# Block-causal attention with a rational feed-forward: q split compactly and placed by transfers, weights rebuilt as float32, four planner numbers

## The chip, the cores and the metric

The kernel runs on one core of a Trainium2 chip. The metric is the device time of one execution in microseconds; times of a version are given as the median of several runs. The engines are PE (TensorE, matmuls; PEld is its weight loading), DVE (VectorE), ACT (ScalarE), POOL (GpSimd) and SP (SyncE), which here only issues the transfers. Each engine works through its own queue of instructions in order.

## The reference, cut to what matters

Attention over 8 batches and 8 heads, 576 tokens, head size 64, with a mask by blocks of 64 tokens; its output, 4608 tokens by 512, goes through a feed-forward with a rational function between two matmuls. All results are float32, and the weights arrive as 64-bit floats.

```
scores = (q @ k.T) / 8, masked where block(i) < block(j)
attn = exp(scores - rowmax) / (rowsum + 1e-9)
x = (attn @ v), heads side by side          # 4608 x 512
h = x @ w_in                                # 4608 x 2048
g = (a0 + a1 h + a2 h^2 + a3 h^3) / (1 + |b0||h| + |b1|h^2 + 1e-6)
out = g @ w_out                             # 4608 x 512
```

## The kernel before

**Precision.** Every float32 operand of a matmul is held as two float32r tiles, a high part (a rounding copy on ACT) and a low part (the rest, by a subtraction on DVE or POOL). A product is three matmuls: high by high, high by low and low by high.

**Attention.** The 64 heads are worked in 32 pairs p. `load` (lines 326 to 341) brings a pair's q, k and v in; `prep` (359 to 385) transposes q and k on PE into a PSUM bank and splits them. For q the two heads go into a block-diagonal tile `qbd` (two of them, alternating), head 0 in partitions 0 to 63 and columns 0 to 63 of each block, head 1 in the other quarter, so that one matmul gives the scores of both heads; the zeros are written once, at lines 316. That takes, for each of q's two parts, an operation of 64 partitions by 512 for each head and a tail of 64 by 64 for each (L348 on ACT for high, L351 on DVE for low). A pair has ten score steps (d, j), ten steps k of a counter that runs through all pairs. At step k `scores` (410) makes the scores on PE and their negative maximum on DVE (L421). `expo` (426), emitted ALAG2 steps later, takes the exponential on ACT (L434), and scales the rows on POOL (L442, L447) after a reciprocal on DVE. `transp` (450), TLAG steps later, transposes the weights of attention on PE (L456) and splits them (L459, L460). `pv` (462), TLAG + 1 and + 2 steps behind a pair's last score step, multiplies with v (L487), rounds the result into the tile `xh` (ACT, L475 and L489) and the rest into `xl` (DVE), moves one half of `xh` across partitions by a transfer into `xt` (L491), adds it on POOL (L494) and stores the two parts to `xscr` in DRAM. For the next pair, OFFS gives the steps behind a pair's first score step at which `load` and the two calls of `prep` are emitted. PSUM has five banks for scores, transposes and results together.

**Weights.** 32 pieces of 128 by 512 are converted by `place` (109 to 140), 20 for the first part of the feed-forward (tiles stay in SBUF) and 12 for the second (high and low parts go to DRAM by L139 and L140 and come back at L583). A piece arrives as pairs of 32-bit words w0, w1. ACT takes the absolute value of w1 as a float (L120), POOL clamps it from below (L121), DVE shifts, masks and joins words in five operations (L123, L125, L128, L129, L130), ACT converts and copies, POOL multiplies.

**Feed-forward.** `Ffn` works 256 tokens at a time in its first part (`ph` 0, ten of the 16 blocks of w_in and w_out, five units a chunk) and 512 tokens in its second. A unit is 24 matmuls with w_in (L198), the rational function on ACT, POOL and DVE (L205 to L231), and 12 or 24 matmuls with w_out (L248). Its input comes back from `xscr` through SP (L181).

**What sets the order.** The program text is emitted step by step: at each attention step the weight pieces due by a table (lines 555, 562), then as many half units as a planner allows. A batch counts as ready `LAST = TLAG + 6` steps after its last step (line 557); the planner spreads the half units linearly up to U1, which is the ready work less HOLD (559, 569). A scheduler of the framework then sorts each engine's queue by its own estimate of times, so the queues do not follow the text exactly. After the last attention step the attention's buffers are freed, the second part's weights are loaded (L583), and the rest of the feed-forward runs alone.

## Time and profile before

| | |
|---|---|
| median of 3 runs | 1394.38 us (1388.48, 1394.38, 1395.79) |
| profiled execution | 1391.85 us, span in the profile 1390.1 us |
| mean granted PE clock | 0.948 |
| busy: PE, PEld | 1264.8 us (91%), 1113.6 us (80%) |
| busy: DVE, ACT, POOL | 1083.2 us (78%), 912.9 us (66%), 959.4 us (69%) |
| DMA | 153.52 MB, 199507 packets, 128480 of them under 512 bytes |

A row of the groups reads: line, engine, operation, output tile <- inputs, shape, count | busy us, mean ns of one | idle time of the engine just before, and what ended it. A row of the waits reads: who waited, for what: us in total, times, longest. Matmuls are pipelined and their ends are modelled, so a busy PE may still not be at its peak. The span falls into an opening without feed-forward, up to about 142 us, a middle in which attention and feed-forward are mixed, a short passage at 970 to 1005 us, and the rest of the feed-forward.

### The profile page before, as it was taken

What the parts mean: (1) busy time and instruction counts of PE and PEld (TensorE: products, weight loads), DVE (VectorE), ACT (ScalarE), POOL (GpSimd) and SP (SyncE); (2) the same over time, 40 slices, a digit from 0 to 9 for tenths busy, and PEclk for the clock granted to TensorE, in tenths of its full rate; (3) what the DMA queues carried; (4) which work ended last, traced back from release to release, by engine and by line L of the source; (5) the groups of instructions that cost most, each with busy time, mean ns of one, the idle gap of its engine ahead of it and who ended that gap; (6) DMA issues with size and microseconds to landing.
All of it is one profiled execution on the core that took longest, in us unless ns stands there. A gap on an engine that the chain in (4) does not pass through costs nothing.

```text
span 1390.1 us, 22425 instructions
## 1 busy us (share of the span) xinstructions
PE 1264.8 (91%) x7352; PEld 1113.6 (80%) x7352; DVE 1083.2 (78%) x2080; ACT 912.9 (66%) x2154; POOL 959.4 (69%) x1080
## 2 busy tenths in 40 slices
PE   6766799899989898999899999999799999999997
PEld 5656688788878787888888889898689888888885
DVE  8999878788777889778887888887287776666674
ACT  6676767676666767668687777776256655565553
POOL 5998867687666777677776777776376655656654
PEclk9776899999999999999999999999899999999998
DMA  5455333345243433334323324322712243333332
GB/s 144 137 148 167 101 100 105 97 115 159 73 121 82 120 105 99 107 88 137 104 77 102 87 67 122 92 80 68 287 31 81 75 134 121 121 122 121 121 113 84
DMA packets 199507, 153.52 MB, mean 110 GB/s; under 512 B 128480, under 2 KB 167392, under 8 KB 199392
## 3 DMA queue, kind: packets, MB, share of 16 engines
q1 hardware_dynamic: 199328, 152.09, 37.6%
q8 instruction: 59, 0.97, 0.3%
q14 instruction: 56, 0.46, 0.1%
q0 software_dynamic: 64, 0.00, 0.0%
HBM read 98.57 MB, written 44.04 MB: 103 GB/s over the span
## 4 chain that ended last, share of the span: by engine, by line
PE 55%; DVE 17%; POOL 10%; ACT 8%; DMA 5%; issue 4%; SPq 1%; POOLq 0%; DVEq 0%; ACTq 0%
PE h L198 21%; PE o L248 20%; PE o L487 5%; PE s L420 4%; PE t L456 2%; DVE ptrl L460 2%; DVE nm L421 2%; POOL p L447 2%; ACT p L434 2%; POOL u L208 2%; DMA xt<-xh 2%; DVE v L222 1%; DVE u L221 1%; DVE s L223 1%; POOL v L207 1%
## 5 line engine op out<-in xcount | busy, mean ns | idle before, releaser
L198 PE MATMUL h<-x,wih 128*128 128x256 f32 (+1 forms) x1872 | 422.6, 316 | 20.2 <-DMA x<-xscr 10.3
L198 PEld LDWEIGHTS h<-x,wih 128*128 128x128 f32 x1872 | 319.1, 196 | 45.1 <-DMA x<-xscr 11.7
L198 PE MATMUL h<-x,wil 128*128 128x256 f32 (+1 forms) x936 | 293.9, 314 | 0.0
L231 POOL TENSOR_TENSOR gl<-s,gh 128x512 fp32r<-128x512 f32 x144 | 189.8, 1319 | 89.4 <-ACT gh L230 88.9
L447 POOL TENSOR_SCALAR p<-p,rc 128x576 f32<-128x576 f32 (+8 forms) x288 | 199.2, 703 | 68.6 <-DVE rc L443 57.5
L248 PE MATMUL o<-woh,gl 128*128 128x512 f32 x576 | 234.0, 406 | 10.5 <-POOL gl L231 10.0
L248 PE MATMUL o<-woh,gh 128*128 128x512 f32 x576 | 229.2, 398 | 0.0
L248 PE MATMUL o<-wol,gh 128*128 128x512 f32 x576 | 228.4, 397 | 0.0
L434 ACT ACTIVATE p<-s,nm 128x288 f32<-128x288 f32 (+4 forms) x320 | 160.4, 505 | 70.3 <-DVE nm L421 42.3
L208 POOL TENSOR_TENSOR u<-v,u 128x512 f32<-128x512 f32 x144 | 191.4, 1329 | 9.5
L198 PEld LDWEIGHTS h<-x,wil 128*128 128x128 f32 x936 | 182.5, 195 | 8.6
L207 POOL TENSOR_SCALAR v<-u,bab 128x512 f32<-128x512 f32 x144 | 122.0, 847 | 94.2 <-ACT u L205 91.8
L421 DVE TENSOR_REDUCE nm<-s 128x1 f32<-128x288 f32 (+4 forms) x320 | 142.7, 450 | 41.8 <-PE s L420 39.6
L209 DVE TENSOR_TENSOR s<-s,h 128x512 f32<-128x512 f32 x144 | 98.3, 683 | 97.7 <-ACT s L206 96.5
L460 DVE TENSOR_TENSOR ptrl<-t,ptrh 128x384 fp32r<-128x384 f32 (+1 forms) x320 | 147.2, 481 | 18.1 <-ACT ptrh L459 16.8
L459 ACT CAST ptrh<-t 128x384 fp32r<-128x384 f32 (+1 forms) x320 | 126.3, 430 | 49.6 <-PE t L456 49.1
L456 PE MATMUL t<-ident,p 128*128 128x128 f32 x800 | 134.5, 291 | 25.0 <-DVE ptrl L460 13.8
L215 ACT ACTIVATE v<-u,qcb 128x512 f32<-128x512 f32 x144 | 104.6, 726 | 74.4 <-POOL u L208 73.7
L230 ACT CAST gh<-s 128x512 fp32r<-128x512 f32 x144 | 89.4, 624 | 87.3 <-DVE s L223 85.1
L205 ACT ACTIVATE u<-h 128x512 f32<-128x512 f32 x144 | 86.2, 599 | 89.7 <-PE h L198 82.7
L248 PEld LDWEIGHTS o<-woh,gl 128*128 128x128 f32 x576 | 110.5, 192 | 33.9 <-POOL gl L231 14.3
L456 PEld LDWEIGHTS t<-ident,p 128*128 128x128 f32 x800 | 100.8, 148 | 43.3 <-issue 7.2
(94 smaller groups left out, 2688.7 us busy)
## 6 DMA issues: line engine op xcount, KB each, us to landing
x<-xscr SPq DMA_DIRECT2D x56, 256.0 KB, 3.7
xt<-xh SPq DMA_DIRECT2D x64, 144.0 KB, 2.4
xscr<-xh SPq DMA_DIRECT2D x64, 144.0 KB, 2.4
xscr<-xl SPq DMA_DIRECT2D x32, 288.0 KB, 2.3
pscr<-os SPq DMA_DIRECT2D x18, 512.0 KB, 2.8
pt<-pscr SPq DMA_DIRECT2D x18, 512.0 KB, 4.2
out_dram<-os SPq DMA_DIRECT2D x18, 512.0 KB, 3.0
qr<-in_q_dram SPq DMA_DIRECT2D x64, 128.0 KB, 2.5
```

The costliest lines, as they stand in the source:

```text
L198: nc.tensor.matmul(h[:, j, :], lhsT=w[:, dc, fs], rhs=xs[dc][:, hl, :], start=(dc == 0 and i == 0), stop=(dc == 3 and i == 2))
L207: nc.gpsimd.tensor_scalar(out=vt, in0=ut, scalar1=b1, scalar2=b0, op0=ALU.mult, op1=ALU.add)
L208: nc.gpsimd.tensor_tensor(out=ut, in0=vt, in1=ut, op=ALU.mult)
L215: nc.scalar.activation(out=vt, in_=ut, func=AF.Ln, bias=qcb)
L231: nc.gpsimd.tensor_tensor(out=gl.rearrange("p j t -> p (j t)"), in0=st, in1=gh.rearrange("p j t -> p (j t)").bitcast(F32), op=ALU.subtract)
L248: nc.tensor.matmul(self.o[m], lhsT=g[:, j, ms], rhs=w[:, f, :], start=(u == 0 and j == 0 and i == 0), stop=(u == nu - 1 and j == NBU[ph] - ...
L421: nc.vector.reduce_max(out=nm[:, j:j + 1], in_=ps[:, :w], axis=AX.X, negate=True)
L434: nc.scalar.activation(out=pts[i][:, c0:c0 + w], in_=s.pop((d, j2))[:, :w], func=AF.Exp, bias=nm[:, n:n + 1], scale=1.0, accum_out=sm[:, j ...
L447: nc.gpsimd.tensor_scalar(out=x, in0=x, scalar1=rc[:, j2:j2 + 1], scalar2=1.0, op0=ALU.mult, op1=ALU.mult)
L456: nc.tensor.transpose(ps[:, x, :], pts[i][:, 128 * kb:128 * kb + 128], ident)
L459: nc.scalar.copy(out=dh, in_=ps[:, :n])
L460: nc.vector.tensor_tensor(out=dl, in0=ps[:, :n], in1=dh.bitcast(F32), op=ALU.subtract)
```

## The change

**q.** For every pair but the first, `prep` writes q's two parts to a compact tile of 128 by 2 by 576 (both heads one above the other, full height), one operation on ACT and one on DVE for the 512 columns and one each for the tail. Two transfers on SP then put the halves of partitions into the block-diagonal tile, 64 partitions by 18 rows of 64 floats each. The compact tile carries the tag "xh" of the attention result, of which there is one buffer: q of a pair and `xh` of the pair two before it follow each other there. The high and low parts of `qbd` become one tile.

**Weights.** The low word's top three bits are joined to the shifted high word, so that the tile holds the weight as a full float32; its high part is then a rounding copy on ACT and its low part a subtraction on POOL. On DVE there are a clamp, one shift with mask and two joins; L128, L129, the conversion on ACT (L132) and the clamp on POOL are gone. In the second part the rounding copy on ACT takes the place of the conversion.

**Numbers.** Exponentials are emitted two steps behind the scores instead of one (ALAG2), transposes seven instead of eight (TLAG, and with it the products with v, and LAST), the two calls of `prep` at steps 2 and 4 instead of 3 and 5 (OFFS), and HOLD is 4 half units instead of 6.

```
-ALAG2 = 1
+ALAG2 = 2
-HOLD = 6
+HOLD = 4
-OFFS = (0, 3, 5)
-TLAG = 8
+OFFS = (0,2,4)
+TLAG = 7
...
             nc.scalar.activation(out=at, in_=w1.bitcast(F32), func=AF.Abs)
-            nc.gpsimd.tensor_scalar_max(at, at, WMIN)
+            nc.vector.tensor_scalar_max(at, at, WMIN)
-            nc.vector.tensor_scalar(out=ai, in0=ai, scalar1=3, scalar2=0x3FFFF000, ...)
-            nc.vector.scalar_tensor_tensor(out=bi, in0=w1, scalar=-0x40000000, in1=ai, ...)
-            nc.vector.tensor_scalar(out=ai, in0=bi, scalar1=-0x800000, scalar2=None, ...)
-            nc.vector.tensor_scalar(out=pi, in0=w0, scalar1=9, scalar2=None, ...)
-            nc.vector.scalar_tensor_tensor(out=pi, in0=w1, scalar=23, in1=pi, ...)
-            nc.scalar.activation(out=pt, in_=pt.bitcast(U32), func=AF.Copy, scale=2.0 ** -43)
+            nc.vector.tensor_scalar(out=ai, in0=ai, scalar1=3, scalar2=0x3FFFFFF8, ...)
+            nc.vector.scalar_tensor_tensor(out=ai, in0=w0, scalar=29, in1=ai, ...)
+            nc.vector.scalar_tensor_tensor(out=ai, in0=w1, scalar=-0x40000000, in1=ai, ...)
             if dt is F32R:
-                nc.scalar.copy(out=dhi, in_=v3(bt))
-                nc.gpsimd.tensor_tensor(out=dlo, in0=v3(pt), in1=v3(at), op=ALU.mult)
+                nc.scalar.copy(out=dhi, in_=v3(at))
+                nc.gpsimd.tensor_tensor(out=dlo, in0=v3(at), in1=dhi.bitcast(F32), op=ALU.subtract)
             else:
-                nc.gpsimd.tensor_tensor(out=v3(pt).bitcast(F32R), in0=v3(pt), in1=v3(at), op=ALU.mult)
+                nc.scalar.copy(out=bt, in_=at)
+                nc.gpsimd.tensor_tensor(out=pt, in0=at, in1=bt.bitcast(F32), op=ALU.subtract)
...
+            if which == 0 and p > 0:
+                s["q"] = att.tile([128, 2, S], F32R, name=f"q{p}", tag="xh", bufs=1)
+                put(s["q"][:, 0, 0:512], s["q"][:, 1, 0:512], ps, QSCALE)
+            elif which == 0:
                 for j in range(2):
                     js = slice(64 * j, 64 * j + 64)
                     put(qh[js, 0:8, js], ql[js, 0:8, js], ps[js].rearrange("p (c t) -> p c t", c=8), QSCALE)
...
+                if p > 0:
+                    for js in halves:
+                        nc.sync.dma_start(out=qbd[p % 2][js, :, :, js].bitcast(F32),
+                                          in_=s["q"][js].rearrange("p x (i t) -> p x i t", t=64).bitcast(F32))
```

The queues change most visibly at two places. The first is the end of attention on PE: the last products with v (`o_1`), and the units behind them (`h_c_u` is unit u of chunk c). Before:

```order
L487 MATMUL o_1_12212<-ptrh,vst 128x192
L487 MATMUL o_1_12212<-ptrl,vst 128x192
L487 MATMUL o_1_12212<-ptrh,vst 128x64
L487 MATMUL o_1_12212<-ptrl,vst 128x64
L198 MATMUL h_14_4_12459<-x_14_0_12076,wih_148 128x256 x2
L198 MATMUL h_14_4_12459<-x_14_0_12076,wil_149 128x256
```

And with the change, at the same place on PE:

```order
L495 MATMUL o_1_12108<-ptrh,vst 128x192
L495 MATMUL o_1_12108<-ptrl,vst 128x192
L495 MATMUL o_1_12108<-ptrh,vst 128x64
L495 MATMUL o_1_12108<-ptrl,vst 128x64
L196 MATMUL h_14_1_12074<-x_14_0_11889,wih_144 128x256 x2
L196 MATMUL h_14_1_12074<-x_14_0_11889,wil_145 128x256
```

Before, units 3 and 4 of chunk 14 were left behind the last attention matmul; now units 1 to 4 are. On SP, a little later, stand the second part's weight loads (`wih`, `wil`, `woh`, `wol`, twelve of 512 KB) and the loads of the last batch's x for chunks 15 and 16. Before:

```order
L495 DMA xscr_77<-xl_12149 128x576
L181 DMA x_15_1_12450<-xscr_76 128x2x192 x2
L181 DMA x_15_1_12450<-xscr_77 128x2x64
L181 DMA x_16_0_12736<-xscr_77 128x2x256 x2
L583 DMA wih_12369<-wih_194 128x4x256
L583 DMA wil_12370<-wil_195 128x4x256
```

With the change, at the other end of the twelve:

```order
L591 DMA wil_12316<-wil_191 128x4x256
L591 DMA woh_12317<-woh_192 128x1024
L591 DMA wol_12318<-wol_193 128x1024
L179 DMA x_15_1_12263<-xscr_76 128x2x192 x2
L179 DMA x_15_1_12263<-xscr_77 128x2x64 x2
L179 DMA x_16_0_12577<-xscr_77 128x2x256 x2
```

Three of the four pieces of `x_15_1` moved from ahead of the weight loads to behind them, where the fourth was already. The second place is ACT in the middle, between the tail of a pair's q and the copy into `xh` (pair numbers are in the names: `tp18` is pair 18, `xh16` pair 16). Before:

```order
L348 ACTIVATE qbd0h_124<-tp18_2_6184 64x64 x2
L348 ACTIVATE k18_6099<-tp18_2_6184 128x64
L220 ACTIVATE v0_6_0_6623<-v0_6_0_6623 128x512
L434 ACTIVATE p1_129,sm17_2_6122<-s17_2_1_6193,nm17_2_6121 128x128
L459 CAST ptrh_122<-t16_4_0_6232 128x3x128
L434 ACTIVATE p5_133,sm17_3_6205<-s17_3_0_6206,nm17_3_6204 128x384
L459 CAST ptrh_122<-t16_4_1_6238 128x2x128
L205 ACTIVATE u0_6_1_6746<-h0_6_1_6721 128x512
L206 ACTIVATE s0_6_1_6748<-h0_6_1_6721,ncoef_104 128x512
L475 CAST xh16_6249<-o16_2_6252 128x2x64
```

With the change, one pair on, from the tail of pair 19's q, which stands in the buffer that `xh17` takes next:

```order
L346 ACTIVATE q19_6386<-tp19_2_6464 128x64
L346 ACTIVATE k19_6380<-tp19_2_6464 128x64
L213 ACTIVATE v0_6_3_6856<-u0_6_3_6855,qcb_108 128x512
L442 ACTIVATE p6_132,sm18_2_6474<-s18_2_0_6475,nm18_2_6473 128x448
L218 ACTIVATE v0_6_3_6856<-v0_6_3_6856 128x512
L467 CAST ptrh_122<-t17_4_0_6508 128x3x128
L467 CAST ptrh_122<-t17_4_1_6514 128x2x128
L442 ACTIVATE p1_127,sm18_2_6474<-s18_2_1_6503,nm18_2_6473 128x128
L442 ACTIVATE p5_131,sm18_3_6521<-s18_3_0_6522,nm18_3_6520 128x384
L228 CAST gh0_6_3_7128<-s0_6_3_6857 128x512
L483 CAST xh17_6565<-o17_2_6568 128x2x64
```

Nine rows stand between q's tail and the copy into the shared buffer here, thirteen for the pair before it. The copy has to wait until both transfers of q have read the buffer.

More of the change, by code (lines that the diff above doesn't have):

```diff
@@ L115, in place @@
             at = ffn.tile([128, 512], F32, name=f"wa{nm}", tag="u")
-            bt = ffn.tile([128, 512], F32, name=f"wb{nm}", tag="v")
-            pt = ffn.tile([128, 512], F32, name=f"wp{nm}", tag="s")
-            ai, bi, pi = at.bitcast(I32), bt.bitcast(I32), pt.bitcast(I32)
+            ai = at.bitcast(I32)
             nc.scalar.activation(out=at, in_=w1.bitcast(F32), func=AF.Abs)
-            nc.gpsimd.tensor_scalar_max(at, at, WMIN)
-            nc.vector.tensor_scalar(out=ai, in0=ai, scalar1=3, scalar2=0x3FFFF000,
+            nc.vector.tensor_scalar_max(at, at, WMIN)
@@ L124, in place @@
+            nc.vector.tensor_scalar(out=ai, in0=ai, scalar1=3, scalar2=0x3FFFFFF8,
                                     op0=ALU.logical_shift_left, op1=ALU.bitwise_and)
-            nc.vector.scalar_tensor_tensor(out=bi, in0=w1, scalar=-0x40000000, in1=ai,
+            nc.vector.scalar_tensor_tensor(out=ai, in0=w0, scalar=29, in1=ai,
+                                           op0=ALU.logical_shift_right, op1=ALU.bitwise_or)
+            nc.vector.scalar_tensor_tensor(out=ai, in0=w1, scalar=-0x40000000, in1=ai,
@@ L133, in place @@
             v3 = lambda x: x.rearrange("p (d f) -> p d f", d=nd)
             if dt is F32R:
-                nc.scalar.copy(out=dhi, in_=v3(bt))
-                nc.gpsimd.tensor_tensor(out=dlo, in0=v3(pt), in1=v3(at), op=ALU.mult)
-            else:
-                nc.gpsimd.tensor_tensor(out=v3(pt).bitcast(F32R), in0=v3(pt), in1=v3(at), op=ALU.mult)
-                nc.sync.dma_start(out=dhi, in_=v3(bt))
-                nc.sync.dma_start(out=dlo, in_=v3(pt))
+                nc.scalar.copy(out=dhi, in_=v3(at))
@@ new lines, in place @@
+                nc.gpsimd.tensor_tensor(out=dlo, in0=v3(at), in1=dhi.bitcast(F32), op=ALU.subtract)
+            else:
+                bt = ffn.tile([128, 512], F32R, name=f"wb{nm}", tag="v")
+                pt = ffn.tile([128, 512], F32R, name=f"wp{nm}", tag="s")
+                nc.scalar.copy(out=bt, in_=at)
+                nc.gpsimd.tensor_tensor(out=pt, in0=at, in1=bt.bitcast(F32), op=ALU.subtract)
+                nc.sync.dma_start(out=dhi, in_=v3(bt).bitcast(F32))
+                nc.sync.dma_start(out=dlo, in_=v3(pt).bitcast(F32))
@@ L311, in attn_ffn_kernel @@
         ptr = [apers.tile([128, 26, 128], F32R, name=f"ptr{x}") for x in "hl"]
-        qbd = [[apers.tile([128, 9, 128], F32R, name=f"qbd{i}{x}") for x in "hl"] for i in range(2)]
+        qbd = [apers.tile([128, 2, 9, 128], F32R, name=f"qbd{i}") for i in range(2)]
         pts = [apers.tile([128, 128 * (i // 2 + 1)], F32, name=f"p{i}") for i in range(9)]
         vst = apers.tile([128, 5, 2, 128], F32R, name="vst")
-        for x in qbd[0] + qbd[1]:
+        for x in qbd:
             nc.vector.memset(x.bitcast(F32), 0.0)
@@ L363, in prep @@
             kh, kl = s["k"][:, 0], s["k"][:, 1]
-            qh, ql = qbd[p % 2]
+            qh, ql = qbd[p % 2][:, 0], qbd[p % 2][:, 1]
             raw = (s["qr"], s["kr"])[which]
@@ L368, in prep @@
                 nc.tensor.transpose(ps[:, 128 * c:128 * c + 128], raw[:, c].rearrange("p j d -> p (j d)"), ident)
-            if which == 0:
+            if which == 0 and p > 0:
+                s["q"] = att.tile([128, 2, S], F32R, name=f"q{p}", tag="xh", bufs=1)
+                put(s["q"][:, 0, 0:512], s["q"][:, 1, 0:512], ps, QSCALE)
+            elif which == 0:
                 for j in range(2):
@@ L377, in prep @@
                 halves = [slice(0, 64), slice(64, 128)]
-                tails = [(qh[js, 8, js], ql[js, 8, js], ps[js, 0:64], QSCALE) for js in halves]
+                if p > 0:
+                    tails = [(s["q"][:, 0, 512:S], s["q"][:, 1, 512:S], ps[:, 0:64], QSCALE)]
+                else:
+                    tails = [(qh[js, 8, js], ql[js, 8, js], ps[js, 0:64], QSCALE) for js in halves]
                 tails.append((kh[:, 512:S], kl[:, 512:S], ps[:, 64:128], 1.0))
                 his = [put_hi(h, x, sc) for h, _, x, sc in tails]
-                for x in his[:2]:
-                    behind(his[2], x)
-                klo = put_lo(*tails[2])
-                for x in tails[:2]:
+                for x in his[:-1]:
+                    behind(his[-1], x)
+                klo = put_lo(*tails[-1])
+                for x in tails[:-1]:
                     behind(put_lo(*x), klo)
+                if p > 0:
+                    for js in halves:
+                        nc.sync.dma_start(out=qbd[p % 2][js, :, :, js].bitcast(F32),
+                                          in_=s["q"][js].rearrange("p x (i t) -> p x i t", t=64).bitcast(F32))
         def vprep(p):
@@ L415, in scores @@
             i, c0, w = DUOS[d][j]
-            qh, ql = qbd[p % 2]
+            qh, ql = qbd[p % 2][:, 0], qbd[p % 2][:, 1]
             kh, kl = s["k"][:, 0], s["k"][:, 1]
```

4 lines of the change are left out of this document (removed).

## Prediction

> **What bounds the kernel now.** I read the busy times by stage first, then the chain of waits in the two halves of the middle, then the groups of instructions in the stage where one engine is full. The columns are the stretch, its length, busy microseconds with instruction counts of PE, PEld, DVE, ACT and POOL, the granted PE clock, the DMA share and GB/s.
>
> ```profile
> span 1390.1 us, 22425 instructions
> 35.00:142.00 107.00, 74.70 (x355) 64.17 (x355) 103.35 (x218) 75.52 (x210) 92.83 (x102) 0.72 0.54 153
> 142.00:560.00 418.00, 374.19 (x2351) 335.32 (x2351) 340.92 (x704) 288.48 (x746) 301.45 (x365) 0.94 0.38 104
> 560.00:970.00 410.00, 394.67 (x2627) 358.72 (x2626) 331.37 (x697) 300.24 (x769) 296.27 (x366) 0.99 0.35 94
> 1005.00:1371.00 366.00, 362.78 (x1736) 305.55 (x1735) 263.72 (x373) 213.62 (x346) 236.08 (x205) 1.00 0.31 103
> ```
>
> Four stages, four limits. In the opening (attention and weight pieces, no feed-forward yet) DVE is busy 103.35 of 107 us: it is the bound, with POOL close behind at 92.83. In the long middle, attention and feed-forward units are mixed, PE has the largest share, and DVE still has 81 to 82%. From 1005 us PE alone decides. The chain of waits says how pure the middle is:
>
> ```profile
> by line: PE h L198 10.7%; PE o L248 9.5%; PE o L487 6.6%; issue 4.8%; PE s L420 4.6%; DMA xt<-xh 3.1%; POOL p L447 3.1%; ACT p L434 3.0%; DVE nm L421 2.9%; DVE ptrl L460 2.7%; DVE v L222 2.6%; POOL u L208 2.5%; DVE s L223 2.3%; POOL xl L494
> by line: PE h L198 19.3%; PE o L248 18.7%; PE o L487 10.1%; PE s L420 8.7%; PE t L456 5.9%; DVE ptrl L460 2.8%; issue 2.5%; DVE nm L421 2.3%; DMA xt<-xh 1.9%; POOL p L447 1.8%; POOL u L208 1.6%; ACT p L434 1.5%; POOL v L207 1.5%; DVE v L222
> ```
>
> The first row is 142 to 560 us: the PE lines listed make 31%. The second is 560 to 970 us: they make 63%. So roughly 0.6 x 418 + 0.35 x 410 = 394 us of the middle hang on other engines, on transfers or on issue, and there the change can act.
>
> **Part 1, weight pieces.** Groups of the opening, 35 to 142 us, then two single clamped-word operations from the timeline, then the clamp on POOL, in the opening as groups and in the middle by stretch:
>
> ```profile
> L123 DVE TENSOR_SCALAR wai<-wai 128x512 int32<-128x512 int32 x7 | 7.1, 1015 | 1.8 <-POOL wai L121 1.7
> L128 DVE TENSOR_SCALAR wao<-wbo 128x512 int32<-128x512 int32 x8 | 4.7, 590 | 0.0
> L129 DVE TENSOR_SCALAR wpi<-sti 128x512 int32<-128x512 int32 x8 | 4.6, 576 | 0.0
> L128 DVE TENSOR_SCALAR wai<-wbi 128x512 int32<-128x512 int32 x7 | 4.2, 598 | 0.0
> L123 DVE TENSOR_SCALAR wao<-wao 128x512 int32<-128x512 int32 x7 | 3.6, 521 | 0.6 <-POOL wao L121 0.5
> L129 DVE TENSOR_SCALAR wpo<-sto 128x512 int32<-128x512 int32 x7 | 3.1, 443 | 0.0
> 28.67 0.41 DVE L123 TENSOR_SCALAR wai<-wai 128x512 int32<-128x512 int32 x1
> 45.51 1.48 DVE L123 TENSOR_SCALAR wai<-wai 128x512 int32<-128x512 int32 x1 [1.71 <-POOL wai L121]
> L121 POOL TENSOR_SCALAR wai<-wai 128x512 f32<-128x512 f32 x7 | 11.4, 1629 | 1.8 <-ACT wai L120 1.8
> L121 POOL TENSOR_SCALAR wao<-wao 128x512 f32<-128x512 f32 x7 | 11.2, 1595 | 0.1
> 142.00:560.00 418.00, 17.89 (x12) 0.94 0.38 104
> 560.00:970.00 410.00, 4.48 (x3) 0.99 0.35 94
> ```
>
> DVE loses L128 and L129, (4.7 + 4.2 + 4.6 + 3.1) / 15 = 1.11 us a piece; the two-operand word operations stay two in number and alike in shape. It gains the clamp. No row shows a clamp on DVE; the nearest is L123, a one-input word operation on the same tile: 0.41 us alone, 1.48 us at worst, (7.1 + 3.6) / 14 = 0.76 us on average, which I take. Net 0.35 us a piece, 14 pieces: -4.9 us, between -9.8 (all at 0.41) and +5.2 (all at 1.48). The 2.4 us for which DVE waited on the POOL clamp go too. POOL loses 11.4 + 11.2 = 22.6 us of its 92.83, so it will not follow DVE as the next bound. A page speaks against the clamp's new place: by the Trainium skill (SBUF — State Buffer, "Who interferes with whom") a DVE operation in a two-port mode and a GpSimd operation lock each other out, and the later one waits for the whole other instruction. The 0.41 and 1.48 us agree; by that rule with a clamp that always comes second, the piece term is the +5.2, and the total below becomes some 10 us less of a gain.
>
> **Part 2, q.** Per pair, one full-height operation and one tail replace two of each:
>
> ```profile
> L351 DVE SCALAR_TENSOR_TENSOR qbd0l<-tp,qbd0h 64x512 fp32r<-64x512 f32 x32 | 21.9, 685 | 1.3 <-ACT qbd0h L348 0.7
> L351 DVE SCALAR_TENSOR_TENSOR k<-tp,k 128x512 fp32r<-128x512 f32 x32 | 21.8, 682 | 2.5 <-ACT k L348 2.3
> ...
> L348 ACT ACTIVATE qbd1h<-tp 64x512 fp32r<-64x512 f32 x32 | 18.9, 592 | 3.9 <-PE tp L368 2.5 <-DVE qbd1l L351 1.1
> ...
> L348 ACT ACTIVATE qbd1h<-tp 64x64 fp32r<-64x64 f32 x32 | 7.0, 218 | 4.1 <-PE tp L376 3.9
> L351 DVE SCALAR_TENSOR_TENSOR qbd0l<-tp,qbd0h 64x64 fp32r<-64x64 f32 x32 | 6.9, 217 | 0.2
> ```
>
> A full-height operation costs what a half-height one does (682 against 685 ns), so a pair saves 685 + 217 ns = 0.90 us on DVE and 592 + 218 ns = 0.81 us on ACT. Four pairs in the opening: -3.6 us. About 26 pairs in the middle: 23.5 us off DVE, 21 off ACT. With the 15 pieces that the clamp's stretches show there, at 0.35 us, DVE loses 28.7 of 340.92 + 331.37 us, 4.3%; ACT loses 3.6%; POOL loses 15 clamps of 1.6 us, 4%. PE's work is the same. If the 394 us off PE shrink by 4%, that is -16 us; bounds 0 (PE covers all) and -33 (4% of 828). I take -14.
>
> **Part 3, the steps.** With TLAG 7 the last transposes, the products with v and a batch's readiness come one step sooner. In the opening
>
> ```profile
> L421 DVE TENSOR_REDUCE nm<-s 128x1 f32<-128x288 f32 (+8 forms) x38 | 16.7, 445 | 0.3
> ```
>
> 38 score steps take 107 us, 2.8 us each: -2.8 for the start of the feed-forward, and -2 at the end of attention, where a step is about as long but partly covered by units; bounds 0 and -2.8 for each. ALAG2 2 holds a score bank one step longer, and leaves the scaling on POOL five steps instead of seven. I price both at nothing, with bounds +10 and -10: the waits of ACT for a maximum become shorter, those of PE for a bank longer. OFFS leaves a load two steps, 5.6 us, before its transposes instead of three; that lead hides it, and if it does not, PE waits up to a step in each pair of the opening, which the same +10 covers.
>
> **Part 4, the end of attention.** Issue times on SP, the chain, and what PE did meanwhile (L198, then L248):
>
> ```profile
> 975.33 2.52 SPq L181 DMA_DIRECT2D x<-xscr  x5
> 979.38 0.58 SPq L583 DMA_DIRECT2D wih<-wih  x1
> ...
> 990.92 0.43 SPq L181 DMA_DIRECT2D x<-xscr  x1
> 990.92 8.23 DMA x<-xscr
> 968.40:999.20 30.80, 10.57 (x85) 10.30 (x84) 0.91 1.00 352
> 968.40:999.20 30.80, 13.35 (x48) 9.87 (x48) 0.91 1.00 352
> 911.72 1.81 PE h L198 x15
> 1091.10 2.72 PE o L248 x12
> ```
>
> PE waits there for the last x, behind twelve weight loads on a full DMA (share 1.00). The last two rows price a matmul: 1.81 / 15 = 0.12 us for L198, 2.72 / 12 = 0.23 for L248. So 85 x 0.12 + 48 x 0.23 = 21 us of work stood in 31 us. In the changed order 120 and 60 such matmuls stand between the last product with v and the first that reads the awaited x: 120 x 0.12 + 60 x 0.23 = 28 us. About 7 us of units move out of the middle into the hole (HOLD by itself would move them the other way; the scheduler's order decides). All of that x now stands behind the weight loads (+1 us of issue). I take -6, bounds -10 and +3.
>
> **Part 5, the new wait.** The q tile and the attention result xh now share one buffer, and q reaches its place by two SP transfers. What is near:
>
> ```profile
> xt<-xh SPq DMA_DIRECT2D x64, 144.0 KB, 2.4
> POOL xl L494 <- DMA xt<-xh: 9.4, 11, 2.0
> SPq L139 <- DVE wbi L125: 31.8, 6, 13.9
> q1 hardware_dynamic: 199328, 152.09, 37.6%
> ```
>
> Added traffic is 31 x 2 x 1152 pieces of 256 bytes, 18.3 MB: by bytes 18.3 / 152.09 x 37.6% = 4.5% of the queue's span, by packet count 71424 / 199328 x 37.6% = 13.5%. In the opening, where the share is 0.54, four pairs add at most 4/31 x 188 = 24 us of 107, so it stays under 0.8. The wait itself is on ACT: its copy into xh stands until both q transfers have landed, with exponentials queued behind; on SP the x loads and the xt transfers are queued behind q's. Between q's tail and that copy stand 9 to 13 ACT rows; at 288.48 / 746 = 0.39 us each, some accumulators and 69% busy, 7 to 10 us. The transfers need about 1 us for the low half on DVE, 1 us of issue and 2.4 us or more to land. Mostly hidden. The nearest row is the POOL wait for a transfer of the same kind, 9.4 us in 32 pairs: I take +10, bounds 0 and +60 (below).
>
> **The sum.** -4.9 - 2.4 - 3.6 - 2.8 (opening) - 14 (middle) - 2 - 6 (end) + 10 = -25.7. The profiled execution took 1391.85 us (its span and 1.75 us around it), so 1366.2; it lies 2.5 us under the median of the three runs, 1394.38, and I forecast **1367 us**. About 7 us, 0.5%, is what a measurement can tell; the three runs themselves lie 1388.48 to 1395.79.
>
> **The rivals.** *PE covers the middle.* The rows of 560 to 970 us speak for it (PE 394.67 of 410), those of 142 to 560 against it. Then the middle gives 0 and the opening, the end and the new wait stay: 1391.85 - 25.7 + 14 = 1380. *The gain is eaten*: with banks held longer (+10) and a covered middle it is 1390, with clamps that always come second (+10) 1400; I put 1393. Speaking for it: DVE has nothing idle in the opening in which a longer clamp could hide. *Slower: the q transfer holds up ACT.* SP serves in order, and the stores of finished weight pieces stand ahead of q in some pairs; such a store waited 31.8 / 6 = 5.3 us on average, 13.9 at most. When q lands more than 7 to 10 us after its tail is written, ACT stops at xh with exponentials and copies behind it, and PE gets neither a free bank nor its transposes' input. At 5 + 5.3 us against the middle cover of 8.5 us that is 2 us a pair, 31 pairs, +60 in place of the +10: 1416. Against it: only 12 of the 32 pieces are stored that way, and SP is idle otherwise. By the Trainium skill (the same page, "Can I just issue two DMAs to hit both halves?") two transfers on separate partition halves gain hardly anything over one after the other; no row here shows a pair of them alone, and by it the landing is 4.8 us and the cover just holds.
>
> **How the numbers follow.** Chances: the sum 0.58 (1367, itself 1340 to 1385), PE covers the middle 0.22 (1380), the gain eaten 0.10 (1393), the ring slower 0.10 (1416). The first two lie over 0.5% below 1394.38, that is under 1387: faster 0.80; same 0.10; slower 0.10. The low end, 1340, is the sum with the middle at -33 and the end at -10. The high end, 1394, takes in the third case and leaves the fourth out.
>
> **What would show it.** Right: DVE in the opening still over 90% but over some 13 us sooner; next to no idle time before the clamp; the two q rows at about 0.68 us; PE at work through the hole; ACT waits for q landings under 15 us in all. Wrong: "ACT xh <- DMA qbd" or "PE s <- ACT p" among the longest waits, or DVE's clamp near 1.5 us. If the stretch from the first unit to the last product with v is no shorter than before, the middle was PE's alone.

## The result and the profile after

The changed kernel took 1331.78 us (median of 4 runs, 1325.76 to 1336.24) against 1391.43 us of the kernel before on the same chip (1386.4 to 1395.79): a ratio of 0.957, 95% interval 0.9512 to 0.9627, 60 us less. The forecast was 1367 us, 25 less, and its range ended at 1340. The sign was right, the size was not. The profiled execution took 1336.24 us, the slowest of the four, with a span of 1334.4.

To find where the 60 us came from I cut both spans at two marks that exist in both: the first VectorE operation of a feed-forward unit, and the last VectorE operation behind a product with v. The columns behind the count are the shortest, median and longest duration in ns, then the first and last start in us. First the kernel before:

```profile
L209 DVE TENSOR_TENSOR s<-s,h x144: 659/686/690, 147.4 to 1369.9; 128x512 f32<-128x512 f32 x144
L490 DVE TENSOR_TENSOR xl<-o,xh x64: 660/689/697, 46.9 to 969.1; 64x512 f32<-64x512 f32 x64
```

and the same two operations after (the feed-forward's lines stand two lower, attention's eight higher):

```profile
L207 DVE TENSOR_TENSOR s<-s,h x144: 666/686/690, 133.9 to 1314.6; 128x512 f32<-128x512 f32 x144
L498 DVE TENSOR_TENSOR xl<-o,xh x64: 661/689/696, 39.2 to 912.1; 64x512 f32<-64x512 f32 x64
```

Now the stretches between the marks, with the columns of the prediction's table by stage (stretch, length, PE, PEld, DVE, ACT, POOL busy, granted clock, DMA share, GB/s), for the kernel before:

```profile
0.00:147.40 147.40, 101.63 (x487) 87.22 (x487) 137.31 (x301) 103.28 (x287) 117.24 (x142) 0.77 0.54 147
147.40:969.10 821.70, 763.61 (x4940) 689.21 (x4941) 666.83 (x1388) 584.58 (x1503) 592.77 (x724) 0.96 0.36 100
969.10:1390.10 421.00, 399.54 (x1927) 337.15 (x1925) 279.10 (x393) 225.00 (x364) 249.36 (x215) 0.98 0.36 119
```

and after:

```profile
0.00:133.90 133.90, 96.58 (x487) 80.95 (x487) 110.78 (x263) 85.47 (x252) 81.84 (x121) 0.81 0.75 183
133.90:912.10 778.20, 740.42 (x4869) 672.61 (x4869) 636.70 (x1320) 559.73 (x1446) 548.98 (x707) 0.97 0.47 125
912.10:1334.40 422.30, 408.39 (x2000) 345.79 (x1998) 288.93 (x402) 231.32 (x376) 253.76 (x221) 0.99 0.36 119
```

The opening is 13.5 us shorter, the middle 43.5, the rest 1.3 longer. But the border between the last two moved. These are the L209 operations ahead of the second mark before:

```profile
0.00:969.10 969.10, 49.73 (x73) 0.93 0.39 107
```

and the L207 operations after:

```profile
0.00:912.10 912.10, 48.45 (x71) 0.95 0.51 133
```

Two units, 24 x 0.12 + 12 x 0.23 = 5.6 us of PE each by the prediction's prices, left the middle and are worked off behind it. At equal units the opening gave 13.5 us, **the middle 32** and the rest 10: the three sum to 55.7, the difference of the spans. The middle itself splits once more: PE's idle time there fell from 58.1 to 37.8 us (20 us), and PE's busy time from 763.6 to 740.4, 12 us more than the two units account for, with the same matmuls, at a granted clock of 0.97 against 0.96.

The chain of waits, over nearly the stretches of the prediction's two rows (130 to 530, 530 to 912 us), points the same way:

```profile
by line: PE h L196 11.6%; PE o L246 11.5%; PE o L495 7.7%; PE s L428 5.6%; issue 5.4%; PE t L464 3.3%; DVE nm L429 3.0%; POOL u L206 2.6%; ACT p L442 2.6%; DVE ptrl L468 2.4%; DMA qbd<-q 2.3%; POOL p L455 2.0%; DMA xt<-xh 2.0%; POOL xl L502
by line: PE o L246 20.6%; PE h L196 19.9%; PE o L495 12.2%; PE s L428 10.8%; PE t L464 6.1%; issue 1.8%; POOL gl L229 1.6%; PE tp L366 1.5%; DVE nm L429 1.5%; ACT p L442 1.5%; POOL xl L502 1.5%; DVE ptrl L468 1.4%; DMA xt<-xh 1.4%; POOL u L
```

The PE lines listed make 40% where they made 31, and 70% where they made 63. By these lists, 0.60 x 400 + 0.30 x 382 = 355 us of the chain now lie on something other than PE, against 0.69 x 418 + 0.37 x 410 = 440 before. (The prediction's 394 put 0.60 and 0.35 for the 0.69 and 0.37, and gave no reason.) That is 85 us less, a fifth and not 4%. The two stretches together are only 46 us shorter: where a wait left the chain, PE's work took over some 39 us of it.

### The profile page after: what moved, and what is told of

Its sections match the earlier page's. It is cut to its first block, busy times and chain, and to the rows that moved or that the text cites. A ratio compares the mean times of both kernels' runs of the same rounds, so it can differ in the third digit from the quotient of the medians.

```text
span 1334.4 us, 22382 instructions
## 1 busy us (share of the span) xinstructions
PE 1245.4 (93%) x7352; PEld 1099.3 (82%) x7352; DVE 1036.4 (78%) x1984; ACT 876.5 (66%) x2072; POOL 884.6 (66%) x1048
## 4 chain that ended last, share of the span: by engine, by line
PE 61%; DVE 12%; ACT 8%; POOL 7%; DMA 6%; issue 4%; SPq 1%; POOLq 0%; DVEq 0%; ACTq 0%
PE h L196 23%; PE o L246 22%; PE o L495 6%; PE s L428 5%; PE t L464 3%; ACT p L442 2%; DMA qbd<-q 2%; DVE nm L429 2%; DVE ptrl L468 2%; POOL u L206 2%; DVE u L219 1%; DVE s L221 1%; ACT ptrh L467 1%; POOL xl L502 1%; POOL p L455 1%
## 5 line engine op out<-in xcount | busy, mean ns | idle before, releaser
L196 PEld LDWEIGHTS h<-x,wih 128*128 128x128 f32 x1872 | 315.6, 194 | 32.2 <-issue 5.8
L455 POOL TENSOR_SCALAR p<-p,rc 128x576 f32<-128x576 f32 (+8 forms) x288 | 186.3, 658 | 57.7 <-DVE rc L451 52.4
L428 PE MATMUL s<-k,qbd 128*128 128x288 f32 (+8 forms) x960 | 197.3, 329 | 16.1 <-DVE ptrl L468 6.2
L428 PEld LDWEIGHTS s<-k,qbd 128*128 128x128 f32 x960 | 159.2, 200 | 34.6 <-ACT p L442 8.2
L205 POOL TENSOR_SCALAR v<-u,bab 128x512 f32<-128x512 f32 x144 | 115.1, 799 | 80.1 <-ACT u L203 76.6
L429 DVE TENSOR_REDUCE nm<-s 128x1 f32<-128x288 f32 (+4 forms) x320 | 140.8, 451 | 34.4 <-PE s L428 32.5
L464 PE MATMUL t<-ident,p 128*128 128x128 f32 x800 | 138.6, 289 | 27.8 <-DVE ptrl L468 10.9
L468 DVE TENSOR_TENSOR ptrl<-t,ptrh 128x384 fp32r<-128x384 f32 (+1 forms) x320 | 149.9, 483 | 18.1 <-ACT ptrh L467 16.5
L207 DVE TENSOR_TENSOR s<-s,h 128x512 f32<-128x512 f32 x144 | 98.4, 683 | 82.3 <-ACT s L204 81.6
```

Of the source, the lines that this page charges most:

```text
L196: nc.tensor.matmul(h[:, j, :], lhsT=w[:, dc, fs], rhs=xs[dc][:, hl, :], start=(dc == 0 and i == 0), stop=(dc == 3 and i == 2))
L205: nc.gpsimd.tensor_scalar(out=vt, in0=ut, scalar1=b1, scalar2=b0, op0=ALU.mult, op1=ALU.add)
L428: nc.tensor.matmul(ps[:, :w], lhsT=x[:, i, :], rhs=y[:, c0:c0 + w], start=(n == 0), stop=(n == 2))
L429: nc.vector.reduce_max(out=nm[:, j:j + 1], in_=ps[:, :w], axis=AX.X, negate=True)
L455: nc.gpsimd.tensor_scalar(out=x, in0=x, scalar1=rc[:, j2:j2 + 1], scalar2=1.0, op0=ALU.mult, op1=ALU.mult)
L464: nc.tensor.transpose(ps[:, x, :], pts[i][:, 128 * kb:128 * kb + 128], ident)
```

## The experiments

Every time is compared with the kernel before on the same chip. Three rounds leave about 4 us of uncertainty either way; the 59.7 us of the changed kernel itself leave 8. The last four columns come from the profiled execution, a single one, in which a mark can lie some microseconds off: the start of the first unit, the middle as it would be with 73 units ahead of its end, the rest as it would be with 71 behind it (5.64 us a unit), and PE's idle time in the middle.

| kernel | median, us | against before | first unit | middle | rest | PE idle |
|---|---|---|---|---|---|---|
| before | 1391.43 | | 147.4 | 821.7 | 421.0 | 58.1 |
| changed | 1331.78 | -59.7 | 133.9 | 789.5 | 411.0 | 37.8 |
| numbers (e1) | 1373.08 | -16.3 | 140.4 | 818.3 | 410.4 | 58.4 |
| q (e2) | 1366.51 | -22.9 | 144.8 | 802.4 | 410.6 | 53.4 |
| weights (e3) | 1353.97 | -35.4 | 141.0 | 797.0 | 413.4 | 44.3 |
| q, weights (e4) | 1357.76 | -31.7 | 138.3 | 784.5 | 430.0 | 41.5 |
| numbers, weights (e16) | 1353.12 | -37.6 | 131.1 | 810.8 | 410.7 | 57.1 |
| numbers, q (e18) | 1360.39 | -29.8 | 143.6 | 799.0 | 411.6 | 48.0 |
| clamp alone (e5) | 1382.89 | -8.0 | 146.1 | 810.3 | 421.7 | 50.9 |
| weights, clamp on POOL (e6) | 1382.72 | -8.1 | 147.4 | 820.2 | 411.6 | 61.5 |
| changed, HOLD 6 (e7) | 1336.63 | -54.2 | 128.4 | 790.1 | 411.3 | 41.5 |
| changed, q sent twice (e8) | 1361.23 | -29.6 | 147.3 | 792.8 | 419.2 | 43.2 |
| changed, DVE more (e9) | 1343.33 | -49.3 | 132.2 | 786.2 | 416.9 | 43.5 |
| changed, ACT more (e10) | 1350.54 | -42.1 | 136.1 | 791.6 | 419.4 | 45.8 |
| changed, POOL more (e11) | 1372.01 | -20.6 | 134.2 | 810.5 | 423.1 | 59.9 |
| changed, PE more (e12) | 1337.98 | -54.7 | 129.3 | 787.7 | 421.4 | 40.8 |
| changed, TLAG 8 (e13) | 1364.53 | -26.2 | 141.4 | 803.2 | 419.7 | 49.9 |
| changed, OFFS (0,3,5) (e14) | 1340.81 | -49.9 | 140.8 | 783.9 | 414.6 | 42.8 |
| changed, ALAG2 1 (e15) | 1332.40 | -58.4 | 132.0 | 786.2 | 412.7 | 37.8 |
| changed, TLAG 6 (e17) | 1361.92 | -28.3 | 135.6 | 804.2 | 417.5 | 50.5 |

How far single executions lie apart can be read from three of these rows. In the changed kernel and in e15 all queues hold the same operations in the same order, but for two neighbours on DVE that change places at about 670 us; in e7 the order is the same up to about 390 us. Yet the first unit started at 133.9, 132.0 and 128.4 us, and where e7's order begins to differ, it was some 11 us ahead. Besides, the profiled execution lies 4.5 us above the median for the changed kernel, and 6.5 and 5.8 us under it for q alone and e9. So a difference of under some 11 us in one of the last four columns shows nothing by itself. The middle's 32 us are well above that (35.5 in e15), though the kernel before has a single profile.

**The parts alone and in pairs (e1 to e4, e16, e18).** Theory A was that the middle shrank because DVE, ACT and POOL have less to do in it; theory B, that the new order relieves waits and PE covers the work removed.

```
e1   before with ALAG2 = 2, HOLD = 4, OFFS = (0,2,4), TLAG = 7
e2   before with the q part: qbd in one tile, put() at full height, the two transfers
e3   before with the weight part: place() of the change
e4   the changed kernel with ALAG2 = 1, HOLD = 6, OFFS = (0,3,5), TLAG = 8
e16  e1 and e3 together;   e18  e1 and e2 together
```

> The kernel before with the four numbers alone (ALAG2 2, HOLD 4, OFFS (0,2,4), TLAG 7); q and the weight pieces as before. Theory A (the middle shrank by 32 us because DVE, ACT and POOL have less to do in it): only the step that comes sooner is left, 2.8 us at each end of attention, and the hole: -3 to -11 us, first feed-forward operation at about 144.5 us. Theory B (the new order relieves waits, the work removed was covered by PE): -25 to -35 us, with the stretch from the first unit to the last product with v shorter by over 20. A mishap of the order by itself (banks held a step longer): up to +10.

> The kernel before with q's part alone: one full-height operation and one tail in place of two of each, and the two transfers. Theory A: 0.90 us less on DVE and 0.81 less on ACT in each of 31 pairs goes through to the end nearly whole: -3.6 in the opening and -15 to -24 in the middle, -18 to -28 in all. Theory B: -3.6 and little else, -5 to +5. By the prediction's own terms (its share of the middle about -11, new wait +10): about -5; if the q transfer holds up ACT: +5 or more, with 'ACT xh <- DMA qbd' among the longest waits.

> The kernel before with the weight pieces alone. All theories: -4.9 and -2.4 in the opening (first feed-forward operation about 7 us sooner). Theory A: another -5 to -8 in the middle (15 pieces, 0.35 us of DVE, 1.6 us of POOL each): -12 to -15 in all. Theory B: -7.

> The changed kernel with the four old numbers (ALAG2 1, HOLD 6, OFFS (0,3,5), TLAG 8): q and weights together, the order of before. Theory A: -40 to -50 of the -60 us. Theory B: -12 to -25. If neither alone does it and the parts need each other (less work in the stages lets the closer order pay), e1 gives -5 to -10, this one -20 to -30, and the two don't add up to -60.

Read the column of the middle first. The numbers alone change it by 3 us, q alone by 19, the weights alone by 25, q and weights by 37. Theory B falls there, and by the time of e1 (-16 where it asked for -25 to -35): the numbers by themselves leave the middle as it was, and it shrinks where work leaves it. Theory A fits e2 alone: e1 gave more than its -3 to -11, the weights far more than its -12 to -15, and q and weights together, -32, less than its -40 to -50. Then the column of the rest. e4 has the shortest middle of all, and 19 us more behind it than the changed kernel. The hole's row of e4, 30 us from the last product with v on, with the columns of the stages:

```profile
928.50:958.50 30.00, 16.99 (x92) 14.49 (x90) 5.01 (x7) 5.04 (x8) 5.99 (x5) 0.88 1.03 358
```

and the same 30 us of the changed kernel:

```profile
912.10:942.10 30.00, 27.05 (x165) 24.57 (x164) 12.84 (x18) 13.28 (x22) 14.73 (x13) 0.94 0.93 326
```

PE works 17 of 30 us in the one and 27 in the other, so part of what q and weights won together was lost again in the hole, and the numbers get it back. Of the 18 us between these two executions, 19 lie behind the last product with v, some 10 of them in these 30 us, and 4 in the opening; the middle gives back 5. By the medians the numbers add 28 us, so a third of their share is not placed.

> The kernel before with the four numbers and the weights' part, q as before. If the parts add up: -16 - 35 = -51. If q is needed for the numbers to pay (or the other way round): -35 to -42. If all three share one gain of the middle that any two of them reach: -45 to -60.

> The kernel before with the four numbers and q's part, weight pieces as before. If parts add up: -16 - 23 = -39. If the numbers pay through q, as with the weights present (-26 on top of q and weights, but -3 on top of the weights alone): -45 to -52. If they don't: -23 to -28.

Neither pair adds up: numbers and weights give 38 and not 51, numbers and q 30 and not 39. One reason stands in the column of the rest: the numbers alone, q alone and the weights alone each shorten it by 8 to 11 us, and so does the whole change. This gain is counted in each part and can be had only once. In e16 the middle is 14 us longer than in e3 and PE's idle time is back at 57 us; why is not settled. So the numbers pay fully only beside both other parts.

**Which half of the weights' part (e5, e6).** One edit each, from the kernel before and from e3:

```diff
e5
-            nc.gpsimd.tensor_scalar_max(at, at, WMIN)
+            nc.vector.tensor_scalar_max(at, at, WMIN)
e6
-            nc.vector.tensor_scalar_max(at, at, WMIN)
+            nc.gpsimd.tensor_scalar_max(at, at, WMIN)
```

> The kernel before with one edit: the clamp of the weight pieces on VectorE instead of GpSimd. The weights' part alone gave -35 us; this tells how much of it is the clamp's place. Theory 1 (GpSimd's 1.6 us in the chain of a piece, and the word operation beside it that it lengthens, are what counts): -15 to -25 us, with the mean of the shift-and-mask operation (L123) falling from 1.34 and 0.91 us in the middle to about 0.5. Theory 2 (the two word operations and the ACT conversion left out are what counts): DVE gets 0.4 to 0.8 us longer a piece, 0 to +8 us.

> The kernel before with the weights' part, but the clamp left on GpSimd. Theory 1: most of the -35 us is lost, -8 to -18 is left. Theory 2: -25 to -35. If the two parts add up, this and the clamp alone make -35.

Each half is worth 8 us, both together 35. Only the first theory's figure for e6 (-8 to -18) is just met, so neither holds as a whole. In e6's profiled execution the first unit and the middle are nearly those of the kernel before, and the rest is some 9 us shorter. What e5 shows is why the clamp is cheap on DVE. The shift-and-mask operation right behind the clamp, over the whole program, in the kernel before (mean ns behind the comma):

```profile
L123 DVE TENSOR_SCALAR wai<-wai 128x512 int32<-128x512 int32 x16 | 16.4, 1027 | 3.2 <-POOL wai L121 2.8
L123 DVE TENSOR_SCALAR wao<-wao 128x512 int32<-128x512 int32 x16 | 11.4, 713 | 3.1 <-POOL wao L121 3.0
```

and in e5, with the clamp (L121) on DVE ahead of it:

```profile
L121 DVE TENSOR_SCALAR wai<-wai 128x512 f32<-128x512 f32 x16 | 11.5, 716 | 0.0
L123 DVE TENSOR_SCALAR wai<-wai 128x512 int32<-128x512 int32 x16 | 10.5, 659 | 0.1
L123 DVE TENSOR_SCALAR wao<-wao 128x512 int32<-128x512 int32 x16 | 10.5, 656 | 0.0
L121 DVE TENSOR_SCALAR wao<-wao 128x512 f32<-128x512 f32 x16 | 9.4, 589 | 0.0
```

The clamp costs DVE 20.9 us, of which the next operation gives back 6.8 and the waits for POOL nearly 6; POOL loses 49.5. Why the two halves are worth 35 together stays open.

**What a microsecond of each engine is worth (e9 to e11).** One operation more in each pair (two in e11), with the same results:

```diff
e9    put(kh[:, 0:512], kl[:, 0:512], ps, 1.0)
+     put_lo(kh[:, 0:512], kl[:, 0:512], ps, 1.0)
e10
+     put_hi(kh[:, 0:512], ps, 1.0)
      put(kh[:, 0:512], kl[:, 0:512], ps, 1.0)
e11   nc.gpsimd.tensor_tensor(out=vl, in0=src, in1=vh.bitcast(F32), op=ALU.subtract)
+     nc.gpsimd.tensor_tensor(out=vl, in0=src, in1=vh.bitcast(F32), op=ALU.subtract)
```

> The changed kernel with k's low half computed twice: 32 more VectorE operations of 0.68 us, 21.8 us in all, five of them before the first feed-forward unit, the rest in the middle; results the same. It measures what a microsecond of VectorE is worth. By the prediction's rate (the opening one for one, the middle half a microsecond for each microsecond off DVE when all three engines shrink together): 3.4 + at most 9, +5 to +12. If VectorE's work is worth nearly its whole length everywhere: +18 to +24. If PE covers the middle: +3 to +4.

> The changed kernel with k's high half copied twice: 32 more ScalarE operations of 0.62 us, 19.7 us in all; results the same. ScalarE is busy 66%, so if only the fullest engine counts: 0 to +3. If the chain of the middle goes through all engines in turn, and a microsecond counts wherever it is removed: +7 to +20.

> The changed kernel with the low half of v computed twice on GpSimd: 64 more operations, 32 of 1.34 us and 32 of 0.51, 59.2 us in all; results the same. If GpSimd is hidden behind the others: 0 to +6. At the rate that the splits so far give (about a third of a microsecond for each microsecond of the three engines together): +15 to +25. One for one: +50 or more.

Against the changed kernel (59.7 us saved) they cost 10.4 us for 21.8 of DVE, 17.6 for 19.7 of ACT and 39.1 for 59.2 of POOL: 0.5, 0.9 and 0.7 us for each microsecond. So "only the fullest engine counts" is wrong here: ACT and POOL, each busy 66%, have a price too. Which of the three is the dearest is not settled, since in the profiled executions the busy time of DVE grew by only 9.9 us, that of ACT by 14.2 and that of POOL by 66.8. The prices are of the whole kernel: behind the last product with v, where none of the added operations stands, the rest grew by 6, 8 and 12 us. In the middle alone only e11 is clear, 21 us for 53 of POOL, or 0.4. And they hold for these places; e5 took 49.5 us off POOL, put 14 on DVE, and gained 8.

**TensorE's clock (e12).**

```diff
+            if p < 5:
+                for n, (x, y) in enumerate(((qh, kh), (qh, kl), (ql, kh))):
+                    nc.tensor.matmul(ps[:, :w], lhsT=x[:, i, :], rhs=y[:, c0:c0 + w], start=(n == 0), stop=(n == 2))
             for n, (x, y) in enumerate(((qh, kh), (qh, kl), (ql, kh))):
```

> The changed kernel with the score matmuls of the first five pairs done twice (10 x 3 matmuls more a pair, some 12 us of TensorE in each, all before or around the first unit); results the same. VectorE bounds the opening. If the granted clock follows how busy TensorE is kept: the clock between 35 and 130 us rises from about 0.75 to over 0.85 and a matmul there gets shorter, and the time moves by -3 to +8. If the clock follows time or load of the chip: it stays at 0.75, TensorE becomes the bound of the opening, +15 to +40.

The opening of the changed kernel and its score matmuls of 288 columns there:

```profile
35.00:130.00 95.00, 69.81 (x358) 58.66 (x357) 81.21 (x187) 60.53 (x180) 62.96 (x86) 0.78 0.75 184
L428 PE MATMUL s<-k,qbd 128*128 128x288 f32 x24 | 5.8, 376 | 2.2 <-DVE ptrl L468 1.3 <-DMA qbd<-q 0.6 <-DVE xl L498 0.3
```

and of e12, where L431 is the same line:

```profile
35.00:130.00 95.00, 79.05 (x483) 70.54 (x482) 86.17 (x196) 65.31 (x191) 64.42 (x92) 0.89 0.72 193
L431 PE MATMUL s<-k,qbd 128*128 128x288 f32 x24 | 4.9, 310 | 0.2 <-ACT p L445 0.2
```

125 matmuls more in this stretch cost 9 us of PE time, where some 12 us in each of five pairs were expected. The granted clock was 0.89 against 0.78, the matmul took 310 ns against 376, and the first unit started 4.6 us sooner. That looks like a clock that follows how busy PE is kept. But the same stretch of e7 and then of e15, with the order of the changed kernel and no matmul added, reads

```profile
35.00:130.00 95.00, 70.78 (x387) 58.26 (x385) 83.61 (x196) 63.46 (x187) 66.77 (x90) 0.86 0.79 199
35.00:130.00 95.00, 68.81 (x373) 56.93 (x371) 81.70 (x188) 61.03 (x182) 65.43 (x88) 0.84 0.78 193
```

One and the same order was granted 0.78, 0.84 and 0.86, and the first unit of e7 (128.4) came before that of e12 (129.3). So e12 shows that redundant matmuls don't delay the opening, and not that they raised the clock: 0.89 is the highest value of all the openings here, but most of the step can be the execution's. The Trainium skill (TensorE: Matmul & The Clock Gate, "What's actually happening") has it that the clock is throttled by default and that activity releases it; 0.89 would fit, and these traces do not settle it. The rest then grew by 10 us, about half of it idle time of PE in the hole, and the whole was 5 us slower.

**The four numbers, one at a time (e7, e13 to e15, e17).** Each is the changed kernel with one number set.

```
e7   HOLD = 6          e13  TLAG = 8         e14  OFFS = (0,3,5)
e15  ALAG2 = 1         e17  TLAG = 6
```

> The changed kernel with HOLD 6 again. q and weights with all four old numbers lost 26 us against the changed kernel, some 18 of it between the last product with v and the end, where PE again waited in the hole (26.6 of 40 us busy, against 37.1). Theory: HOLD decides how many units are kept for the hole, and 6 instead of 4 leaves it emptier: +8 to +15 us against the changed kernel, units after the last product with v fewer than 73. Rival: the order of loads on the transfer queue decides (OFFS, TLAG), HOLD changes nothing there: 0 to +3.

> The changed kernel with TLAG 8 again (transposes, products with v and a batch's readiness a step later). By the prediction's terms: +2.8 in the opening and +2 at the end of attention, +5. If the step is what fills the hole after attention (q and weights with the old numbers had 18 us more there): +15 to +25, most of it after the last product with v.

> The changed kernel with OFFS (0, 3, 5) again (the transposes of q, k and v of the next pair at the old steps). By the prediction's terms 0, within 3. Rival: with the old places k's or q's transposes wait for a bank beside the products of the pair before, once a pair: +8 to +20, spread over the middle.

> The changed kernel with ALAG2 1 again (the exponentials one step after their scores, not two). Theory: with one step ACT meets a maximum that DVE hasn't finished ('ACT p <- DVE nm' was 35.5 + 21.6 us in the middle of the kernel before), with two it doesn't: +6 to +15 in opening and middle, the wait back above 30 us. Rival, by the prediction: 0, since a score bank held a step longer costs PE what ACT gains.

> The changed kernel with TLAG 6. If a shorter lag is better by itself (TLAG 8 to 7 gave -33): another -5 to -20. If it is the step on which things fall (with TLAG 8 the transposes of p lie on odd steps, with 7 on even ones, as q's and k's do): back by +10 to +30. A third way: q's transfer then has two steps instead of three until ACT's copy into the shared buffer, and the wait 'xh <- DMA qbd' (12.2 us) grows to 30 or more, +10 or more.

ALAG2 is not tested by e15 (+1.3 us): the scheduler arrives at the same order with 1 as with 2, as said above, so with the other numbers changed this one hardly reaches the queues. HOLD leaves the hole as it is (411.3 against 411.0) and makes +5.5, about what three rounds can tell. OFFS makes +9.8, just clear of the uncertainty, and not in the middle, where the rival had put it. TLAG decides: +33.5 with 8, +31.4 with 6. So a shorter lag is not better by itself. It is a place that suits the other steps, and a step off on either side costs the same. For 6 the waits show something: these are the waits of the transposes of p and of ACT's copy, in the changed kernel (total us, times, longest)

```profile
ACT xh L483 <- DMA qbd<-q: 12.2, 12, 1.9
PE t L464 <- DVE ptrl L468: 10.9, 9, 3.2
PEld t L464 <- issue: 3.1, 6, 0.9
```

and in e17:

```profile
PEld t L464 <- issue: 19.5, 18, 2.8
PE t L464 <- DVE ptrl L468: 17.7, 12, 3.6
ACT xh L483 <- DMA qbd<-q: 17.2, 14, 3.0
```

They grow by 5 to 16 us each, not by 31, and lie on three queues side by side. That both 8 and 6 put the transposes of p on the odd steps of a pair would also fit; the runs don't tell a crowded step from a lag that is too short.

**The new wait (e8).** Each transfer of q is issued twice:

```diff
+                    for _ in range(2):
                         for js in halves:
                             nc.sync.dma_start(out=qbd[p % 2][js, :, :, js].bitcast(F32),
```

> The changed kernel with each of q's transfers issued twice (18.3 MB more, about 1 us more issue on SP for a pair, the second pair lands later, ACT's copy into the shared buffer waits for it). If q's transfers are on the chain with their whole wait, a pair costs 3 to 5 us more: +60 or more over 31 pairs, and the prediction's +10 for the first copy was real. If they are hidden behind the 7 to 10 us between q's tail and that copy: 0 to +12, with the ACT wait 'xh <- DMA qbd' growing from 12.2 us to 30 or more without the time following it one for one.

It cost 30 us against the changed kernel, between the two cases. The first unit came 13.4 us later (147.3), the rest grew by 8, and the middle, with some 26 of the 31 pairs, by 3. ACT's wait for q did not grow as the second case had it; in this kernel the wait stands on the transfer queue, where the second copy waits for the first:

```profile
SPq L393 <- DMA qbd<-q: 74.4, 49, 3.7
ACT xh L484 <- DMA qbd<-q: 5.8, 8, 1.2
```

So the second pair of transfers is nearly hidden in the middle and costs about 3 us a pair in the opening, where a step has no feed-forward beside it. The chain of waits of the changed kernel agrees. In its opening, 35 to 130 us, q's landings are the largest entry:

```profile
by line: DMA qbd<-q 14.7%; PE o L495 8.2%; issue 8.1%; DVE ptrl L468 7.1%; DMA sto<-in_moe_w_out_dram 5.9%; DVE nm L429 5.4%; PE t L464 5.2%; DMA sti<-in_moe_w_in_dram 4.9%; PE s L428 4.0%; ACT p L442 3.4%; PE tp L366 3.0%; DVE xl L498 2.9%
```

That is 14 of 95 us (22.8% in e15, 25.6% in e7), against 2.3% between 130 and 530 us. How much of it a kernel without these transfers would save is not shown.

## Why the prediction was wrong, point by point

The profiled spans differ by 55.7 us, 30 more than the 25.7 of the sum. Of these 30, 18 are the middle (32 against 14), 10 the charge for the new wait, which is contained in the measured stretches, and 2 the end (10 against 8).

**The opening: the sum near, the reason only partly.** Forecast -13.7 us, measured -13.5, in part by luck: e15 and e7, with the same order there, make it -15.4 and -19.0. The weights alone moved the first unit by 6.4 us (forecast 4.9 + 2.4), q alone by 2.6 (3.6), the numbers alone by 7.0 (2.8). They overlap, and none is far above what single executions differ by. The 20 conversions on ACT (L132) that fall away, 0.63 us each, stand in no term. The clamp's price, taken from L123 as 0.76 us, was too high in the opening, to which these two rows belong:

```profile
L119 DVE TENSOR_SCALAR wao<-wao 128x512 f32<-128x512 f32 x7 | 3.1, 441 | 4.6 <-ACT wao L118 4.6
L119 DVE TENSOR_SCALAR wai<-wai 128x512 f32<-128x512 f32 x6 | 2.8, 472 | 2.1 <-ACT wai L118 2.1
```

and too low in the middle:

```profile
L119 DVE TENSOR_SCALAR wai<-wai 128x512 f32<-128x512 f32 x7 | 10.0, 1435 | 0.0
L119 DVE TENSOR_SCALAR wao<-wao 128x512 f32<-128x512 f32 x8 | 7.4, 921 | 0.0
```

"DVE in the opening still over 90%" was wrong: it is busy 81.21 of 95 us, 85%, with the DMA share at 0.75 (forecast under 0.8). DVE is no longer what holds the opening: q's landings have the largest share of the chain there (e8), where the prediction had called the new wait mostly hidden.

**The middle: the step that failed.** Part 2 said: "If the 394 us off PE shrink by 4%, that is -16 us", and took -14. The load was sized well. At equal units (a unit has about 3.9 us of DVE, 3.4 of ACT and 3.4 of POOL, an estimate from the means of its lines in the middle), DVE lost 22 us there (forecast 28.7), ACT 18 (21) and POOL 37 (24): 77 us against 74. What failed is the exchange rate. 14 / 74 is 0.19 us for each microsecond of the three engines; 32 / 77 is 0.42, with the new wait's cost already in it. Read the same way, q alone gives 0.28, the weights alone 0.48, both 0.40, and POOL work added (e11) 0.4; with the new numbers and one part it is 0.25 (e16) and 0.95 (e18), so this is no constant. The proportional rule had two faults. It let a stage shrink only by the share of load that leaves it, as if each engine's part of the chain were a stock of its own; why a microsecond counts for 0.4 and not for 0.2 is not shown beyond these rates. And it held PE's time fixed ("PE's work is the same"): the work is the same, but the 12 us less of busy PE are part of the 32. In every kernel with q's part or the whole weights' part, PE is busy 10 to 23 us less in the middle at equal units, with the numbers alone 4. That shorter waits raise the clock would explain it, but it is an argument from the clock of 0.97 against 0.96 and from the count of matmuls; e12 does not show it.

**The four numbers, the second step that failed.** "I price both at nothing, with bounds +10 and -10": for ALAG2 that came out because the order hardly changed with it, not because a bank's wait and a maximum's wait cancelled; OFFS, which the same +10 was to cover, lies at its very edge (9.8). TLAG was allowed a step at each end, 4.8 us in all, and is worth 33 beside q and weights; in the profiled execution with TLAG 8, 7.5 of it stand in the opening, 14 in the middle and 9 behind it. So the middle's 32 us are won by the work that left, but only with an order that suits it. A lag was priced by how far it moves its own operation, not by what it comes to stand beside.

**The hole.** Forecast -6 with bounds -10 and +3; it gave 10, two units more behind the last product with v in nearly the same time. The reason was right in kind, but not particular to the whole change: the numbers alone and q alone have the same rest. That HOLD would work against it is not borne out: with 6 the hole is the same.

**The new wait.** Forecast +10. ACT waited 12.2 us for q's landings (under the 15 that were named), POOL 9.3 for xt (9.4 before). The pair landed after 4.3 us, near the 4.8 that the prediction worked out for two one after the other, but no run sends one half alone. The cost is not measured by itself: e8 shows that the copy is nearly hidden in the middle, where q alone still gains 19 us, and the chain puts what is left into the opening. The rival of the ring is refuted, and so is "PE covers the middle": the stretch that this rival keeps as it was is 32 us shorter at equal units.

## What to carry to other kernels

Where several engines of 65 to 80% load pass work round a ring beside PE, don't price removed work by its share of a stage: measure the rate first by adding one harmless operation on each engine, since here it was 0.5 to 0.9 us of the whole for a microsecond added, and not nothing for the engines that are less full. Take two profiles of the same order before you read a stage to a few microseconds: here they lay up to 11 us apart. Lags and offsets in an order written out by hand belong to the work they stand between, so try them again after that work has changed, one at a time and both ways, and see whether the number reaches the queues at all. Parts that don't add up (16, 23 and 35 us make 75, together they gave 60) are no reason to distrust the sum; look for the stage whose gain each part wins alone and all together only once, as the hole here.

## What the runs showed of the hardware

- The granted TensorE clock between 35 and 130 us was 0.78, 0.84 and 0.86 in three executions of the same order (changed kernel, e15, e7), and 0.89 with 125 redundant matmuls (e12). No wait of PE listed in that stretch of the changed kernel was longer than 3.2 us.
- A one-input VectorE operation on 128x512 words took 0.44 to 0.47 us on average in the opening and 0.92 to 1.44 in the middle, for the same clamp in the same program; the operation behind it took 1.03 and 0.71 us with the clamp on GpSimd and 0.66 with it on VectorE.
- q's transfers, 288 KB each in pieces of 256 bytes and issued two at a time, landed 4.3 us after issue (median of 62; the longest 8.5), against 2.3 us for the 144 KB of xt:

```profile
qbd<-q SPq DMA_DIRECT2D x62, 288.0 KB, 4.3
xt<-xh SPq DMA_DIRECT2D x64, 144.0 KB, 2.3
```
